# Attention ahead of two feed-forward stages: the weighted sums of half a sequence begin eight steps behind its first scores instead of nine

## The chip, the cores and the metric

The kernel runs on one core of a Trainium2 chip. The metric is the device time of one execution in microseconds (us); lower is better. Before the change the median of three runs is 1412.94 us (1412.52 to 1413.05).

## What is computed

Two batches of 768 tokens with 8 heads of 64 go through attention with a causal window of 128 keys and 4 sink keys, then through a dense feed-forward stage (512 to 2048 to 512), then through a mixture of eight experts (512 to 1024 to 512 each) whose weights come from a softmax that is balanced in eight rounds. Cut to what matters:

```python
scores = scale * np.matmul(q, k.transpose(0, 1, 3, 2))
scores = np.where(is_sink | in_window, scores, -1e9)
a = np.exp(scores - scores.max(-1)); a = a / (a.sum(-1) + 1e-9)
x = np.matmul(a, v)                      # attention, then to (1536, 512)
h = x @ w_in
x = (h * sigmoid(h)) @ w_out             # dense stage
P = balanced softmax of x @ w_gate       # eight rounds
out = sum over e of P[:, e] * (relu(x @ w1[e]) @ w2[e])
```

Only the attention and its passage into the dense stage are touched by the change; they fill about the first 160 us of the span.

## The kernel before

**Units, halves, steps.** Attention works on 8 units (a batch and a pair of heads) of 6 query tiles of 128 rows, so on 48 tiles in all (`NS`). Three consecutive tiles are a half, w = 0 to 15; a half is half of a unit's sequence, and even halves (g = 0) have three groups of keys, odd ones (g = 1) four. The loop at L325 in `banded` runs over steps s. Each step records, for several tiles at different stages, the instructions that all engines then run in the order recorded; no scheduler reorders them, and an engine that waits holds up everything recorded behind the wait on that engine.

**What a step records.** For tile s the scores of both heads on PE (`scores`, L236) and, on DVE, mask and row maximum (L240, two instructions and their read-outs). For tile s-1 the exponentials on ACT (L248). Then the weighted sums of an older half (`weighted`), one of its three parts per step. For tile s-2 the normalisation (`normalise`: L253 and L255 on DVE, L257 on POOL). For tile s-4 the transposes of the probabilities on PE (`turn`, L270). Where s is a multiple of 3, one more set of transposes for the sink keys of half s/3-2 (`turn_sinks`, L280). What PE wrote is then split in a high part (`highs`, ACT, L308) in the same step and a low part (`lows`, DVE, L313) in the next step; from step 48 on both come in the same step. The tiles are `tp` to `pt` for the probabilities, `ts` to `ss` for the sinks, `pv` to `xH` and `xL` for the result.

**The weighted sums.** Part 0 of half w opens an accumulation bank with the sinks' product (L292, which reads the whole of `ss`, high and low) and goes on with 6 matmuls (even halves) or 12 (odd halves) of 128x256; parts 1 and 2 have 6 each, and part 2 closes with the second sinks' product (L302). Each group of three matmuls (L111, L112, L113) is high by high, high by low, low by high. They read the values `vz`, which POOL splits four times per unit (`values`, L222 and L224), the first unit's at steps 4 to 7. Before the change part p of half w stands in step 3w+9+p.

**Beside it.** Steps 0 to 7 also record four idle transposes that keep PE at work (`warm_up`, L96). The generator `timeline` (L990) adds the preparation of the dense stage's weights: eight half chunks, each decoded over seven steps from step 7+5i on (`decode`, DVE L540, L541, L543; ACT L535, L545, L554; POOL L536, L547, L548, L555), and, around step 48, chunks of the second weight matrix. From step 48 on it also records blocks of the dense stage (`first`, tiles `pa`, twelve matmuls of 128x512, then L636 on ACT, L637 and L640 on DVE): blocks 0 to 3 of the first 512 tokens at steps 48 to 51, and blocks 0 to 2 of the second 512 tokens later. The latter read `xH` and `xL` of half 14, so they stand behind its part 2. With each block the planner's tasks go one stage on, and these put the decoding of the second matrix's chunks on DVE's queue between the blocks' own instructions.

```python
if s >= 9:
    late += weighted((s - 9) // 3, ii)
```

Of the kernel before, what the change touches and what calls it, by code (L numbers as in the profile page):

```python
# [26 lines left out]
def attn_ffn_moe_kernel(ctx, tc, q, k, v, n_sink, window, w_in, w_out, w_gate, w1, w2, out):  # L27
# [3 lines left out]
    NT = S // 128  # L31
# [19 lines left out]
    NU = len(units)  # L51
# [42 lines left out]
    def warm_up(ps, n):  # L94
        for _ in range(n):
            nc.tensor.transpose(ps[:, 0:128], ident, ident)  # L96
# [13 lines left out]
    def three(ps, sH, sL, mH, mL, first, last, **kw):  # L110
        nc.tensor.matmul(ps, sH, mH, start=first, stop=False, **kw)  # L111
        nc.tensor.matmul(ps, sH, mL, start=False, stop=False, **kw)  # L112
        nc.tensor.matmul(ps, sL, mH, start=False, stop=last, **kw)  # L113
# [35 lines left out]
    def banded(sp, experts):  # L149
# [36 lines left out]
        def masks():  # L186
            nc.vector.tensor_scalar(kp[:, prev], it[:, prev], wd, None, ALU.is_lt)
            nc.vector.tensor_scalar(mk[:, 1, own], kp[:, own], -1.0, -NEG, ALU.add, ALU.mult)
            nc.vector.tensor_tensor(mk[:, 1, prev], kp[:, prev], snk, ALU.max)
            yield  # L190
            nc.vector.tensor_scalar(mk[:, 1, prev], mk[:, 1, prev], -1.0, -NEG, ALU.add, ALU.mult)
            yield
            nc.vector.tensor_copy(kp[:, 128 : 128 + SK], snk[:, 0:SK])
            nc.vector.tensor_scalar(mk[:, 2], kp, -1.0, -NEG, ALU.add, ALU.mult)
# [32 lines left out]
        def scores(s):  # L227

            u, i = divmod(s, NT)
            res = []  # L230
            ps = [sp.bank(f"sc{s}_{h}", "sc")[:, :KW] for h in range(2)]
            qs = slice(128 * i, 128 * i + 128)
            ks = slice(160 * max(i - 1, 0), 160 * max(i - 1, 0) + KW)
            for h in range(2):
                d = slice(64 * h, 64 * h + 64)
                nc.tensor.matmul(ps[h], rq[u % 2][d, qs], rk[u % 2][d, ks], start=True, stop=True)  # L236
            for h in range(2):
                ng = ngs[(2 * s + h + 4) % 6]
                nm = sp.small.tile([128, 1], F32, name=f"nm{s}_{h}", tag="nm")
                nc.vector.tensor_tensor_reduce(ng, ps[h], mk[:, min(i, 2)], -SCALE, 3.0e38, ALU.add, ALU.min, nm)  # L240
                res.append((ng, nm))
            logits[s] = res

        def exponentials(s):
            pr = prs[s % 7]
            sm = sp.small.tile([128, 2], F32, name=f"sm{s}", tag="sm")
            for h, (ng, nm) in enumerate(logits.pop(s)):
                nc.scalar.activation(pr[:, :, h], ng, AF.Exp, bias=nm, scale=-1.0, accum_out=sm[:, h : h + 1])  # L248
            probs[s] = (pr, sm)

        def normalise(s):
            pr, sm = probs[s]
            nc.vector.tensor_scalar(sm, sm, 1.0e-9, None, ALU.add)  # L253
            yield
            nc.vector.reciprocal(sm, sm)  # L255
            for h in range(2):
                nc.gpsimd.tensor_scalar(pr[:, :, h], pr[:, :, h], sm[:, h : h + 1], 1.0, ALU.mult, ALU.mult)  # L257
# [26 lines left out]
        def weighted(w, part):  # L284

            u, g = divmod(w, 2)
            b, hp = units[u]
            pH, pL = pt[g]
            ms = [[[0], [1], [2]], [[0, 1], [2], [3]]][g][part]
            if part == 0:  # L290
                pos[w] = sp.bank(f"pv{w}", "pv")[:, :384]
                nc.tensor.matmul(pos[w], vs[0][:, u], sinks[w], start=True, stop=False)  # L292
            po = pos[w]
            for m in ms:
                j, t0 = prods[g][m]
                for h in range(2):
                    vH, vL = (x[:, j, 64 * h : 64 * h + 128] for x in vz[u % 2])
                    mH, mL = (x[:, h, 2 * m : 2 * m + 2].rearrange("p a b -> p (a b)") for x in (pH, pL))
                    three(po[:, 128 * t0 : 128 * t0 + 256], vH, vL, mH, mL, False, False, skip_group_check=True)
            if part < 2:  # L300
                return []
            nc.tensor.matmul(po, vs[1][:, u], sinks.pop(w), start=False, stop=True)  # L302
            c = slice(b * S + 384 * g, b * S + 384 * g + 384)
            return [(xH[hp][:, c], xL[hp][:, c], pos.pop(w))]
# [16 lines left out]
        NS = NT * NU  # L321
        late = []
        vals = iter(())
        setup = masks()
        for s in range(NS + 9):  # L325
            w, ii = divmod(s, 3)
            parts, late = late, []
            if s < NS:
                scores(s)
            if s < 8:  # L330
                warm_up(sp.bank("wt", "tr"), 4)
            next(setup, None)
            next(setup, None)
            if 0 <= s - 1 < NS:
                exponentials(s - 1)
            if s >= 9:
                late += weighted((s - 9) // 3, ii)
            nrm = normalise(s - 2) if 0 <= s - 2 < NS else iter(())
            next(nrm, None)
            lows(parts)  # L340
            next(nrm, None)
            if 0 <= s - 4 < NS:
                late += turn(s - 4)
            if ii == 0 and 0 <= w - 2 < 2 * NU:
                late += turn_sinks(w - 2)
            highs(late)
            if s >= NS:
                lows(late)
                late = []
            if s in (3, 4):  # L350
                c = slice(4 * s - 12, 4 * s - 8)
                nc.scalar.copy(vs[0][:, c], vsr[:, c])
                nc.gpsimd.tensor_tensor(vs[1][:, c], vsr[:, c], f32(vs[0][:, c]), ALU.subtract)
            if (s == 4 or s > 2 and s % 6 == 2) and s // 6 < NU:
                vals = values(s // 6)
            next(vals, None)
            if s % 6 == 0 and 0 < s and s // 6 + 1 < NU:
                load_unit(s // 6 + 1, "kq")
            if (s == 8 or s > 5 and s % 6 == 5) and s // 6 + 2 - (s == 8) < NU:
                load_unit(s // 6 + 2 - (s == 8), "v")  # L360
            next(experts)
# [609 lines left out]
    with tc.If(rvl != 0) as cmp:  # L971
        with tc.manual_schedule(), ExitStack() as st:
            sp = Space(st)
            ex = Experts(sp)
            ex.plan(True)

            halves = [words(sp.vsr, 512 * i, 512) for i in range(2)]
            tmp = [[words(sp.tm, 512 * i + 256 * c, 256) for c in range(2)] for i in range(2)]

            def load_half(i):  # L980
                c = 256 * (i // 2)
                nc.sync.dma_start(halves[i % 2].bitcast(I32).rearrange("p (k f) -> p k f", k=2), w_in.bitcast(I32)[:, c : c + 256].rearrange("(k p) f -> p k f", p=128)[:, 2 * (i % 2) : 2 * (i % 2) + 2])

            def decode_half(i):
                o = [words(t, 256 * (i % 2), 256, F32R) for t in ex.buffer("A", 0, i // 2)]
                yield from ex.decode(halves[i % 2], tmp[i % 2], o, True)
                if i + 2 < 8:
                    load_half(i + 2)

            def timeline():  # L990
                gens = {}
                for s in range(NT * NU + 9):
                    if s == 5:
                        load_half(0)
                        load_half(1)
                    for i in range(8):
                        at = s - 7 - 5 * i
                        if at == 0:
                            gens[i] = decode_half(i)
                        if at in (0, 1, 2, 3, 4, 5, 6):  # L1000
                            next(gens[i], None)
                    at = s - NT * NU
                    for a in (-6, -1, -1, 0):
                        if at == a:
                            ex.fetch()
                    if at == -3:
                        gens["Z"] = ex.prepare("Z", 0, 0)
                    if -3 <= at <= 1:
                        next(gens["Z"], None)
                    if at in (0, 1, 2, 3, 6, 7, 8):  # L1010
                        next(blocks)
                    yield

            blocks = ex.run(True)
            banded(sp, timeline())
            sp.cycle = ["sc"] * 3 + ["tr"] * 3
            for _ in blocks:
                pass
# [51 lines left out]
```

## Time and profile before

| what | value |
|---|---|
| median of the runs shown | 1412.94 us (1412.52 to 1413.05) |
| profiled execution: its own time | 1414.62 us |
| profiled execution: its span | 1412.8 us (1.8 us lie around it) |
| PE busy | 1399.0 us, 99% |
| DVE, ACT, POOL busy | 856.3, 537.0, 504.2 us (61, 38, 36%) |
| share of the chain of waits on PE | 96% |
| mean granted clock of PE | 0.996 |
| PE's waits over 0.5 us after the start | xL 2.2 us, once; vz L791 1.6 us, once; vz L790 1.0 us, twice |

How to read it: the span is that of the one execution that was profiled; the busy time of PE is modelled, because matmuls overlap, so a PE that looks busy may still be held up by short waits. In a timeline each line has the start, the length, the engine, the line of the kernel, what is written from what, how many instructions were merged, and in brackets how long the engine was idle before and what ended that. The distance from one PE line to the next is the time that its instructions really take up.

### The profile page before, as it was taken

The numbers are of one execution on the slowest core, as the hardware profiler recorded it, in microseconds if no ns is written. First come the engines' busy times: TensorE is split into PE (matmuls) and PEld (weight loads), VectorE is DVE, ScalarE is ACT, GpSimd is POOL, SyncE is SP. The second block draws the span as 40 slices with busy tenths as digits, with TensorE's granted clock in tenths as the row PEclk, the third lists the DMA queues.
The fourth block names the chain that finished last, engine by engine and source line by source line (L and its number), as shares of the span: only waits on it lengthen the run. The fifth ranks groups of instructions, "written<-read, shape, count | busy, mean of one in ns | idle before, by whom it ended". The sixth has DMA issues, their size and how long they took to land.

```text
span 1412.8 us, 18980 instructions
## 1 busy us (share of the span) xinstructions
PE 1399.0 (99%) x7065; PEld 1223.7 (87%) x7065; DVE 856.3 (61%) x1645; ACT 537.0 (38%) x1241; POOL 504.2 (36%) x657
## 2 busy tenths in 40 slices
PE   9999999999999999999999999999999999999998
PEld 6778788888878899989998998899899989989997
DVE  7989798786565756555455455545554554555454
ACT  6887333333345333333333333333333333332330
POOL 7887232232223233234333223432322343233230
PEclk9999999999999999999999999999999999999999
DMA  5341122211000100001000100100010011001002
GB/s 132 112 126 67 60 77 73 75 60 61 16 15 31 45 29 32 31 30 45 30 30 33 43 30 31 45 31 30 30 46 30 31 34 42 31 30 46 15 0 92
DMA packets 60293, 65.29 MB, mean 46 GB/s; under 512 B 10400, under 2 KB 47520, under 8 KB 60192
## 3 DMA queue, kind: packets, MB, share of 16 engines
q1 hardware_dynamic: 59904, 63.99, 14.0%
q8 instruction: 57, 0.93, 0.3%
q14 instruction: 44, 0.36, 0.1%
q10 hardware_dynamic: 288, 0.00, 0.0%
HBM read 60.84 MB, written 3.15 MB: 45 GB/s over the span
## 4 chain that ended last, share of the span: by engine, by line
PE 96%; DVE 1%; DMA 1%; POOL 1%; ACT 0%; SPq 0%; issue 0%; ACTq 0%; DVEq 0%
PE py L113 13%; PE py L112 12%; PE py L111 12%; PE pq L111 11%; PE pq L113 11%; PE pq L112 11%; PE pz L111 3%; PE pz L113 3%; PE pz L112 3%; PE pa L112 3%; PE pa L113 3%; PE pa L111 3%; PE sc L236 2%; PE tp L270 1%; PE pv L111 1%; PE pv L113 1%
## 5 line engine op out<-in xcount | busy, mean ns | idle before, releaser
L834 DVE SCALAR_TENSOR_TENSOR pr<-py,P,pr 128x512 f32<-128x512 f32 x224 | 168.1, 750 | 117.8 <-PE py L113 117.8
L113 PE MATMUL py<-pt,vz 128*128 128x512 f32 x576 | 226.2, 393 | 1.6 <-DVE vz L791 1.6
L111 PE MATMUL py<-pt,vz 128*128 128x512 f32 x576 | 225.2, 391 | 1.0 <-ACT vz L790 1.0
L112 PE MATMUL py<-pt,vz 128*128 128x512 f32 x576 | 225.5, 392 | 0.0
L787 DVE TENSOR_TENSOR mk<-pq,rqk 128x384 f32<-128x384 f32 x128 | 71.3, 557 | 214.4 <-PE pq L113 214.4
L571 POOL TENSOR_TENSOR pt<-ng,pt 128x256 fp32r<-128x256 f32 (+1 forms) x66 | 66.3, 1009 | 210.9 <-ACT pt L570 210.9
L571 POOL TENSOR_TENSOR pt<-rqk,pt 128x512 fp32r<-128x512 f32 (+1 forms) x50 | 55.0, 1101 | 225.6 <-ACT pt L570 225.5
L113 PEld LDWEIGHTS py<-pt,vz 128*128 128x128 f32 x576 | 108.3, 188 | 25.5 <-DVE vz L791 2.7
L111 PEld LDWEIGHTS py<-pt,vz 128*128 128x128 f32 x576 | 108.3, 188 | 21.9 <-ACT vz L790 1.6
L112 PEld LDWEIGHTS py<-pt,vz 128*128 128x128 f32 x576 | 108.2, 188 | 19.9
L794 ACT COPY rqk<-pq 128x384 f32<-128x384 f32 x64 | 30.7, 480 | 216.2 <-PE pq L113 216.2
L790 ACT ACTIVATE vz<-mk 128x384 fp32r<-128x384 f32 x128 | 66.9, 522 | 80.5 <-DVE mk L787 80.5
L791 DVE SCALAR_TENSOR_TENSOR vz<-mk,vz 128x384 fp32r<-128x384 f32 x128 | 72.0, 562 | 6.0 <-ACT vz L790 6.0
L112 PE MATMUL py<-pt,ss 128*128 128x512 f32 x192 | 74.9, 390 | 0.0
L111 PE MATMUL py<-pt,ss 128*128 128x512 f32 x192 | 74.6, 389 | 0.0
L636 ACT ACTIVATE mk<-pa 128x512 f32<-128x512 f32 x48 | 28.7, 598 | 101.3 <-PE pa L113 63.5
L834 DVE SCALAR_TENSOR_TENSOR tm<-py,P,tm 128x512 f32<-128x512 f32 x56 | 42.0, 751 | 32.6 <-PE py L113 32.6
L637 DVE TENSOR_TENSOR mk<-mk,pa 128x512 f32<-128x512 f32 x48 | 33.0, 687 | 43.0 <-ACT mk L636 42.9
L112 PE MATMUL pa<-xL,wa 128*128 128x512 f32 x144 | 56.7, 393 | 2.2 <-DVE xL L313 2.2
L257 POOL TENSOR_SCALAR pr<-pr,sm 128x288 f32<-128x288 f32 x96 | 51.9, 557 | 16.0 <-DVE sm L255 6.0
L570 ACT CAST pt<-ng 128x256 fp32r<-128x256 f32 (+1 forms) x66 | 33.5, 509 | 63.2 <-POOL ng L585 24.9
L111 PE MATMUL pa<-xH,wa 128*128 128x512 f32 x144 | 57.0, 396 | 0.0
(428 smaller groups left out, 3807.6 us busy)
## 6 DMA issues: line engine op xcount, KB each, us to landing
rqk<-in_moe_w_dram SPq DMA_DIRECT2D x32, 512.0 KB, 3.3
rv<-in_moe_w_dram SPq DMA_DIRECT2D x16, 512.0 KB, 3.4
ng<-in_moe_w_dram SPq DMA_DIRECT2D x16, 512.0 KB, 3.2
rqk<-in_moe_w_out_dram SPq DMA_DIRECT2D x8, 512.0 KB, 3.2
rv<-in_v_dram SPq DMA_DIRECT2D x8, 384.0 KB, 3.7
rqk<-in_moe_w_in_dram SPq DMA_DIRECT2D x6, 512.0 KB, 3.8
rqk<-in_k_dram SPq DMA_DIRECT2D x7, 384.0 KB, 5.1
rqk<-in_q_dram SPq DMA_DIRECT2D x7, 384.0 KB, 5.4
```

The source lines that it names most:

```text
L111: nc.tensor.matmul(ps, sH, mH, start=first, stop=False, **kw)
L112: nc.tensor.matmul(ps, sH, mL, start=False, stop=False, **kw)
L113: nc.tensor.matmul(ps, sL, mH, start=False, stop=last, **kw)
L257: nc.gpsimd.tensor_scalar(pr[:, :, h], pr[:, :, h], sm[:, h : h + 1], 1.0, ALU.mult, ALU.mult)
L570: nc.scalar.copy(o[0], src)
L571: nc.gpsimd.tensor_tensor(o[1], src, f32(o[0]), ALU.subtract)
L637: nc.vector.tensor_tensor(sg, sg, ps, ALU.mult)
L787: add = lambda o, x, y: nc.vector.tensor_tensor(o, x, y, ALU.add)
L790: nc.scalar.activation(oH, src, AF.Relu)
L791: nc.vector.scalar_tensor_tensor(oL, src, 0.0, f32(oH), ALU.max, ALU.subtract)
L794: nc.scalar.copy(self.p1, ps)
L834: nc.vector.scalar_tensor_tensor(o, ps, self.P[:, tt, e : e + 1], o, ALU.mult, ALU.add)
```

## The change

The loop over steps ends at step 55 instead of 56. Part p of half w moves from step 3w+9+p to step 3w+8+p. In `timeline` the three blocks of the second 512 tokens move from the 6th, 7th and 8th step after step 48 to the 5th, 6th and 7th.

```diff
-        for s in range(NS + 9):
+        for s in range(NS + 8):
...
-            if s >= 9:
-                late += weighted((s - 9) // 3, ii)
+            if s >= 8:
+                late += weighted(*divmod(s - 8, 3))
...
-                for s in range(NT * NU + 9):
+                for s in range(NT * NU + 8):
...
-                    if at in (0, 1, 2, 3, 6, 7, 8):
+                    if at in (0, 1, 2, 3, 5, 6, 7):
                         next(blocks)
```

No instruction is added or removed on any engine; SP's queue of transfers stands in the same order. PE and, with the results, ACT and DVE get another order. Three places on PE (names: `sc8_0` are the scores of tile 8 for head 0, `tp4` the transposes of tile 4, `pv0` the sums of half 0, `ss` the sinks; the number at the end is a buffer's).

Steps 8 and 9, where the sums begin, before:

```order
L236 MATMUL sc8_0_422<-rqk1_73 128x288
L236 MATMUL sc8_1_423<-rqk1_73 128x288
L270 MATMUL tp4_438<-ident_84,pr_155 128x128 x4
L236 MATMUL sc9_0_446<-rqk1_73 128x288
L236 MATMUL sc9_1_447<-rqk1_73 128x288
L292 MATMUL pv0_457<-ss_162,vs_159 128x384
L111 MATMUL pv0_457<-pt0_160,vz0_156 128x256
L112 MATMUL pv0_457<-pt0_160,vz0_156 128x256
L113 MATMUL pv0_457<-pt0_160,vz0_156 128x256
```

and now (the three matmuls per head stand twice, for two heads; the first head's are shown):

```order
L236 MATMUL sc8_0_422<-rqk1_73 128x288
L236 MATMUL sc8_1_423<-rqk1_73 128x288
L292 MATMUL pv0_433<-ss_162,vs_159 128x384
L111 MATMUL pv0_433<-pt0_160,vz0_156 128x256
L112 MATMUL pv0_433<-pt0_160,vz0_156 128x256
L113 MATMUL pv0_433<-pt0_160,vz0_156 128x256
...
L270 MATMUL tp4_446<-ident_84,pr_155 128x128 x4
L236 MATMUL sc9_0_454<-rqk1_73 128x288
L236 MATMUL sc9_1_455<-rqk1_73 128x288
```

The first part of half 0 has moved ahead of the transposes of tile 4 and the scores of tile 9.

The end of half 0 and the start of half 1, as it recurs for each half, before:

```order
L302 MATMUL pv0_457<-ss_162,vs_159 128x384
L270 MATMUL tp7_537<-ident_84,pr_155 128x128 x4
L236 MATMUL sc12_0_548<-rqk0_72 128x288
L236 MATMUL sc12_1_549<-rqk0_72 128x288
L292 MATMUL pv1_559<-ss_162,vs_159 128x384
```

and now:

```order
L302 MATMUL pv0_433<-ss_162,vs_159 128x384
L270 MATMUL tp6_514<-ident_84,pr_155 128x128 x2
L236 MATMUL sc11_0_522<-rqk1_73 128x288
L236 MATMUL sc11_1_523<-rqk1_73 128x288
L292 MATMUL pv1_533<-ss_162,vs_159 128x384
```

The sinks' product of half 1 stands behind the scores of tile 11 instead of those of tile 12, while the sinks it reads are still made by DVE between its work on tiles 10 and 11.

Around block 2 of the dense stage (`pa0_0_2`), before:

```order
L270 MATMUL tp46_1943<-ident_84,pr_155 128x128 x4
L111 MATMUL pa0_0_2_1952<-xH0_64,wa_149 128x512
...
L113 MATMUL pa0_0_2_1952<-xH3_67,wa_149 128x512
L292 MATMUL pv14_1975<-ss_162,vs_159 128x384
...
L270 MATMUL tp47_1983<-ident_84,pr_155 128x128 x4
```

and now:

```order
L292 MATMUL pv14_1945<-ss_162,vs_159 128x384
...
L270 MATMUL tp46_1953<-ident_84,pr_155 128x128 x4
L111 MATMUL pa0_0_2_1960<-xH0_64,wa_149 128x512
...
L113 MATMUL pa0_0_2_1960<-xH3_67,wa_149 128x512
```

Part 0 of half 14 has moved ahead of block 2. On DVE the order from this block's L637 to the low part of half 14's result (`xL_71`) and on is the same as before.

## Rows read from the trace of the kernel before

**Rows 1.** The page, part 1: busy us, share of the span, instructions.

```profile
PE 1399.0 (99%) x7065; PEld 1223.7 (87%) x7065; DVE 856.3 (61%) x1645; ACT 537.0 (38%) x1241; POOL 504.2 (36%) x657
```

**Rows 2.** Timeline of PE, steps 8 and 9: start us, length us, instruction, idle before.

```profile
23.52 0.76 PE L236 MATMUL sc<-rqk 64*128 64x288 f32 x4
...
26.05 0.44 PE L292 MATMUL pv<-ss,vs 128*128 128x384 f32 x1
...
27.36 0.39 PE L113 MATMUL pv<-pt,vz 128*128 128x256 f32 x1 [0.29 <-POOL vz L224]
27.59 0.66 PE L270 MATMUL tp<-ident,pr 128*128 128x128 f32 x4
```

**Rows 3.** Timeline of POOL, the split of the first unit's values, second head.

```profile
24.81 0.53 POOL L222 TENSOR_SCALAR vz<-rv 128x384 fp32r<-128x384 f32 x1
...
26.28 1.03 POOL L224 TENSOR_TENSOR vz<-rv,vz 128x384 fp32r<-128x384 f32 x1
```

**Rows 4.** Timeline of PE, steps 10 to 12.

```profile
28.50 0.76 PE L236 MATMUL sc<-rqk 64*128 64x288 f32 x4
29.19 0.39 PE L111 MATMUL pv<-pt,vz 128*128 128x256 f32 x1
...
30.01 0.41 PE L270 MATMUL tp<-ident,pr 128*128 128x128 f32 x2
30.35 0.76 PE L236 MATMUL sc<-rqk 64*128 64x288 f32 x4
31.04 0.38 PE L111 MATMUL pv<-pt,vz 128*128 128x256 f32 x1
...
32.03 0.63 PE L270 MATMUL tp<-ident,pr 128*128 128x128 f32 x4
32.58 0.76 PE L236 MATMUL sc<-rqk 64*128 64x288 f32 x4
33.27 0.44 PE L292 MATMUL pv<-ss,vs 128*128 128x384 f32 x1
```

**Rows 5.** Timeline of DVE, step 10: scores to sinks of half 1.

```profile
29.29 0.46 DVE L240 CUSTOM_DVE_ANT_0 ng<-sc,mk 128x288 f32<-128x288 f32 x1 [0.50 <-PE sc L236]
...
30.05 0.17 DVE L253 TENSOR_SCALAR sm<-sm 128x2 f32<-128x2 f32 x1
...
30.84 0.55 DVE L313 TENSOR_TENSOR ss<-ts,ss 64x384 fp32r<-64x384 f32 x1
```

**Rows 6.** Timelines of PE, POOL and DVE, steps 40 and 41: half 11.

```profile
103.16 0.76 PE L236 MATMUL sc<-rqk 64*128 64x288 f32 x4
...
102.89 1.00 POOL L224 TENSOR_TENSOR vz<-rv,vz 128x384 fp32r<-128x384 f32 x1
...
103.21 0.71 DVE L253 TENSOR_SCALAR sm<-sm 128x2 f32<-128x2 f32 x1
...
104.54 0.55 DVE L313 TENSOR_TENSOR ss<-ts,ss 64x384 fp32r<-64x384 f32 x1
```

**Rows 7.** Timeline of PE, scores of step 42.

```profile
105.40 1.26 PE L236 MATMUL sc<-rqk 64*128 64x288 f32 x4
```

**Rows 8.** Timeline of PE: behind block 2, and the first block of the second tokens.

```profile
133.32 0.33 PE L292 MATMUL pv<-ss,vs 128*128 128x384 f32 x1
...
134.21 0.65 PE L270 MATMUL tp<-ident,pr 128*128 128x128 f32 x4
...
145.66 0.50 PE L112 MATMUL pa<-xL,wa 128*128 128x512 f32 x1 [2.20 <-DVE xL L313]
```

**Rows 9.** Timeline of DVE: block 2's L637, and half 14's low part.

```profile
134.15 0.69 DVE L637 TENSOR_TENSOR mk<-mk,pa 128x512 f32<-128x512 f32 x1 [0.92 <-ACT mk L636]
...
145.06 0.55 DVE L313 TENSOR_TENSOR xL<-pv,xH 128x384 fp32r<-128x384 f32 x1
```

**Rows 10.** Busy us by stretch: PE, PEld, DVE, ACT, POOL, granted clock, DMA share, GB/s.

```profile
146.50:150.00 3.50, 3.50 (x13) 2.92 (x12) 2.88 (x4) 2.18 (x4) 2.33 (x2) 0.51 0.00 0
```

## Prediction

> **What bounds the kernel now.** I first read the table of engines on the page: PE is busy for 1399.0 us, 99% of the span [rows 1], and every other engine far less. The change removes no instruction, so it can win only what PE idles, and it loses whatever new idle time it makes. Then I read PE's timeline over the attention, to see where PE waits and for whom. Three places matter. At the start of the sums, in step 9, the sixth matmul of half 0 waits for POOL's last split of the values: it starts at 27.36, right behind the split's end at 26.28 + 1.03 = 27.31 [rows 2, 3]. In between, PE runs one instruction behind the other; the time of a piece is the distance between starts: scores 0.69, part 1 of a half 0.82, two transposes 0.34, part 2 of a half 0.99, four transposes 0.55 [rows 4]. Last, behind the mixed blocks, PE stands still for 2.20 us until DVE delivers half 14's low part [rows 8], and right after that the granted clock is 0.51 for 3.50 us [rows 10], which is the lower of its levels, 1.2 GHz. DVE's timeline tells why DVE is late there: it had waited 0.92 us before block 2's L637 at 134.15, worked from then on without a gap, and came to `xL` at 145.06 [rows 9]. So that stall's end is set by DVE's queue, counted from block 2.
>
> **The change part by part.**
>
> *The start of the sums: 1.24 us lost.* Part 0 of half 0 now stands in step 8, behind scores that start at 23.52 [rows 2]. It can begin at 23.52 + 0.69 = 24.21. Its second head needs the high values, ready at 24.81 + 0.53 = 25.34, and the last matmul needs the low values, ready at 27.31 [rows 3]. POOL's queue up to there holds only work on tiles whose scores came earlier, so it doesn't move. PE therefore ends part 0 at 27.59, as before. But before, the transposes of tile 4 and the scores of tile 9 were done by then, and now they come after: 0.55 + 0.69 = 1.24 us. Nothing hides this, as PE runs on without a gap afterwards. DVE gets tile 9's scores later too, and uses the time on nothing that PE waits for.
>
> *The start of each later half: 2.2 us lost (0.8 to 3.7).* L292 of half w reads `ss`, which DVE finishes behind the scores of tile 3w+7. For half 1 these scores start at 28.50, and `ss` is done at 30.84 + 0.55 = 31.39 [rows 4, 5]. Before, L292 came at 33.27 [rows 4], 1.88 us later. Now it stands behind the scores of tile 11, started at 30.35, and part 2 (0.99) has taken the place of part 1 (0.82) before it: 30.35 + 0.69 + 0.17 = 31.21, which is 0.18 us too early. The same reckoning over halves 1 to 13, each on its own rows, gives 4.15 us in all. Half 1 is the first of them, half 11 the worst: 103.16 + 0.86 = 104.02 against 104.54 + 0.55 = 105.09, 1.07 us short [rows 6]. Where DVE isn't behind, the odd halves are short by 0.18 as half 1 is and the even ones by nothing, so seven odd halves make 1.26 us. The rest is DVE being behind on decoding, and a wait on PE gives DVE time to catch up. Also, where DVE was behind, PE had paid already at the next scores, 1.26 - 0.76 = 0.50 us at step 42 [rows 7], and needn't pay twice. Bounds: 1.26 - 0.50 = 0.76 and 4.15 - 0.50 = 3.65. I take the middle, 2.2, because part of the lag goes. Behind the waiting L292 stand the matmuls of part 0, the transposes and the next scores, so DVE and ACT wait for it too.
>
> *Why DVE's pace is uncertain.* The small L253 ahead of `ss` took 0.17 us in step 10 and 0.71 in step 40 [rows 5, 6]; in the latter, POOL's L224 ran from 102.89 to 103.89 and L253 ended at 103.92 [rows 6]. The Trainium skill, page "SBUF — State Buffer", section "Who interferes with whom", says that the vector engine in a two-port mode and GpSimd exclude each other for a whole instruction, whoever is first. The trace agrees with it in that pair.
>
> *The tail: 0.89 us lost.* Part 0 of half 14 has moved ahead of block 2: from 133.32 to 134.21, 0.89 us [rows 8]. Block 2 ends that much later, and DVE's queue from block 2's L637 to `xL` stands in the same order, 145.06 + 0.55 - 134.15 = 11.46 us of work without a gap [rows 9]. The 0.92 us that DVE waited there grows, and `xL` comes 0.89 later. PE has less to do before it, so its stall grows from 2.20 to about 3.1 us. What PE does after the stall is the same as before. The step that falls away had no time of its own: its part of the sums is only run elsewhere.
>
> *The clock: 0.85 us lost (0 to 1.7).* The stall of 2.20 us was followed by 3.50 us at 0.51, which costs 0.49 x 3.50 = 1.7 us [rows 10]. The tail's stall should be followed by the same, so that costs nothing new; its bounds are 1.7 us either way, should it fall while PE stands or last twice as long. The new stall in step 8 is about 2.1 us in two pieces, the longer from about 25.6 to 27.36. It is a bit shorter than the row's and broken by two matmuls, so I take half of 1.7.
>
> *At nothing:* the three blocks of the second tokens, which keep their place behind half 14 and beside half 15; the earlier results `xH` and `xL`, which nobody waits for before step 48; transfers, in the same order. If DVE had been the bound in the attention, the earlier `xL` would shift its load too, but over three steps DVE does the same work.
>
> *Sum.* 1.24 + 2.2 + 0.89 + 0.85 = 5.2 us. The profiled execution took 1414.62 us (span 1412.8), 1.7 above the median of 1412.94. So it would be 1419.8 profiled, and 1412.94 + 5.2 = 1418.1 as a median, 0.37% slower. From about 160 us on PE works without slack, so nothing later takes it back.
>
> **The rivals.** (A) *The waits are absorbed.* DVE catches up after the first stall, L292 costs only the lower bound of 0.76, and the clock doesn't fall in step 8: 1.24 + 0.76 + 0.89 = 2.9 us; should the tail's fall in clock then cost 1 us less, 1414.8. For it: every wait of PE hands DVE time. Against it: DVE's path from scores to `ss` is latency, 31.39 - 28.50 = 2.89 us [rows 4, 5], which no slack shortens.
>
> (B) *Faster.* PE's rows look dense because the model stretches matmuls, and the steps are in truth paced by the other engines, each running ahead of PE by a step. Then a step less is a step's time less: 30.35 to 32.58, 2.2 us [rows 4], and half 14's low part comes before PE asks for it, which saves 2.20 and the 1.7 of the clock: 1412.94 - 6.1 = 1406.8. It decides at DVE: had DVE no gap before block 2's L637, its queue would be the pace, and `xL` would come earlier with the earlier step. The row shows a gap of 0.92 [rows 9], which speaks against it.
>
> (C) *Collisions on every half.* If PE's new rhythm puts L253 behind POOL each time, each of 13 halves pays 0.71 - 0.17 = 0.54 [rows 5, 6], 7.0 us more: 1425.1. The rule of the skill named above would make it so where POOL's instruction is always first. For it is that POOL and DVE then run in lockstep with PE; against it, that in step 10 POOL didn't hold L253 up.
>
> That the change doesn't do what it says is excluded: the order on PE shows the moved parts.
>
> **How the numbers follow.** Forecast 0.66, A 0.22, B 0.08, C 0.04. A measurement of this kernel can tell about 0.2% from no change, 2.8 us, so faster is below 1410.1 and slower above 1415.8. Forecast and C lie above, A on the whole within, B below: faster 0.08, same 0.22, slower 0.70. The forecast's own range goes from its lower bounds, 1.24 + 0.76 + 0.89 = 2.9, less 1.7 for the tail's clock, 1414.1, to its upper ones, 1.24 + 3.65 + 0.89 + 1.7 = 7.5 and 1.7 more for a longer fall in the tail, 1422.1. That takes in A, and leaves out B and C.
>
> **What would show it.** Right: L113 of half 0 waiting for `vz` L224 by about 1.7 us and ending at about 27.6; L292 waiting for `ss` at odd halves; the wait for `xL` with block 2's L637 behind an idle DVE. Wrong: no wait at L292, scores of step 42 starting at 105.40 or before [rows 7], or a stall for `xL` under 2.2 us.

## The result, and the profile after

The changed kernel takes 1420.96 us, the median of five runs (1419.93 to 1422.22). Beside it the kernel before took 1413.05 us (1412.52 to 1414.32). The ratio is 1.0055, with a 95% interval of 1.0044 to 1.0066: 0.55% slower, 7.9 us. The forecast of 1418.1 us had the sign, and its range of 1414.1 to 1422.1 holds the time; the cost was 7.9 us where 5.2 were worked out. The profiled execution took 1421.31 us, its span 1419.4.

The page of the changed kernel, the busy table and the first line of the chain of waits:

```profile
PE 1398.2 (99%) x7065; PEld 1223.0 (86%) x7065; DVE 858.1 (60%) x1645; ACT 536.5 (38%) x1241; POOL 503.9 (35%) x657
...
PE 94%; DVE 3%; DMA 1%; ACT 1%; issue 0%; SPq 0%; POOL 0%; ACTq 0%; DVEq 0%
```

The busy times are those of [rows 1]. On the chain of waits PE has lost 2 points of its 96%, and DVE stands there now with 3%. The list of PE's waits says for what (total us, times, longest us):

```profile
PE pv L292 <- DVE ss L313: 6.0, 10, 1.2
PE pa L112 <- DVE xL L313: 2.3, 1, 2.3
PE py L113 <- DVE vz L791: 1.6, 1, 1.6
...
PE pv L113 <- POOL vz L224: 1.4, 1, 1.4
...
PE pv L111 <- POOL vz L222: 0.4, 1, 0.4
```

The first line is new: L292 never waited over 0.5 us before. The wait for `xL` and the one for `vz` L791 were there before; the waits for L224 and L222 are those of step 8. The timeline of PE shows where they lie, here steps 8 to 11, and L292 of two later halves:

```profile
23.54 0.76 PE L236 MATMUL sc<-rqk 64*128 64x288 f32 x4
24.23 0.44 PE L292 MATMUL pv<-ss,vs 128*128 128x384 f32 x1
...
25.41 0.39 PE L111 MATMUL pv<-pt,vz 128*128 128x256 f32 x1 [0.40 <-POOL vz L222]
...
27.35 0.40 PE L113 MATMUL pv<-pt,vz 128*128 128x256 f32 x1 [1.44 <-POOL vz L224]
...
32.07 0.76 PE L236 MATMUL sc<-rqk 64*128 64x288 f32 x4
...
35.18 0.44 PE L292 MATMUL pv<-ss,vs 128*128 128x384 f32 x1 [0.36 <-DVE ss L313]
...
50.59 0.45 PE L292 MATMUL pv<-ss,vs 128*128 128x384 f32 x1 [0.97 <-DVE ss L313]
...
111.46 0.44 PE L292 MATMUL pv<-ss,vs 128*128 128x384 f32 x1 [1.16 <-DVE ss L313]
```

Three things differ from [rows 2] and [rows 4]. The last matmul of part 0 of half 0 still starts at 27.35, but PE stood before it for 1.44 us and 0.40 us. The scores of step 10 start at 32.07 instead of 28.50. And L292 waits for `ss` at its half: 0.36 us at half 1, 0.97 at half 3, 1.16 at half 11.

The first window below gives a part of why step 10 is so late: by its granted clock, PE ran at 0.52, the lower of its levels, 1.2 GHz, right after the stall in step 8. The second window is the one behind the stall in the tail, and answers to [rows 10]. Columns as in [rows 10].

```profile
27.50:31.00 3.50, 3.50 (x14) 2.41 (x15) 1.09 (x6) 1.64 (x5) 1.78 (x4) 0.52 0.40 112
153.50:157.50 4.00, 3.66 (x12) 3.20 (x13) 2.05 (x4) 2.25 (x4) 1.19 (x1) 0.57 0.00 0
```

The tail, DVE's timeline, then PE's stall, which answer to [rows 9] and [rows 8]:

```profile
142.34 0.69 DVE L637 TENSOR_TENSOR mk<-mk,pa 128x512 f32<-128x512 f32 x1 [1.28 <-ACT mk L636]
...
153.24 0.55 DVE L313 TENSOR_TENSOR xL<-pv,xH 128x384 fp32r<-128x384 f32 x1
```

```profile
153.84 0.77 PE L112 MATMUL pa<-xL,wa 128*128 128x512 f32 x1 [2.26 <-DVE xL L313]
```

Block 2's L637 is 8.19 us later than before and `xL` 8.18: DVE's queue between the two is the same length, as forecast. So all of the loss has been made by then. Where it was made can be counted on the starts of PE's scores:

- up to step 10: 32.07 - 28.50 = 3.57 us. Of this, 0.82 is part 1 of half 0, which now lies ahead of that point and is no loss. 2.75 us are.
- from step 10 to step 47: the scores there start at 125.11 instead of 117.94, 7.17 later. 0.99 is part 2 of half 12, moved ahead likewise. So 6.18 - 2.75 = 3.43 us were lost at halves 1 to 12.
- half 13: its L292 waits 0.97 us at 126.83, and some 0.1 more goes in starting again.
- block 2: 0.89, by the move alone.

The sum is 2.75 + 3.43 + 1.07 + 0.89 = 8.1 us, and the first matmul of the dense stage's second product starts 8.12 us later, at 165.76 instead of 157.64.

### The profile page after: what moved, and what is told of

It reads as the page before. It is cut to its first block, busy times and chain, and to the rows that moved or that the text cites. A ratio compares the mean times of both kernels' runs of the same rounds, so it can differ in the third digit from the quotient of the medians.

```text
span 1419.4 us, 18979 instructions
## 1 busy us (share of the span) xinstructions
PE 1398.2 (99%) x7065; PEld 1223.0 (86%) x7065; DVE 858.1 (60%) x1645; ACT 536.5 (38%) x1241; POOL 503.9 (35%) x657
## 3 DMA queue, kind: packets, MB, share of 16 engines
HBM read 60.84 MB, written 3.15 MB: 45 GB/s over the span
## 4 chain that ended last, share of the span: by engine, by line
PE 94%; DVE 3%; DMA 1%; ACT 1%; issue 0%; SPq 0%; POOL 0%; ACTq 0%; DVEq 0%
PE py L113 12%; PE py L112 12%; PE py L111 12%; PE pq L111 11%; PE pq L113 11%; PE pq L112 11%; PE pz L112 3%; PE pz L111 3%; PE pz L113 3%; PE pa L112 3%; PE pa L113 3%; PE pa L111 3%; PE sc L236 1%; PE tp L270 1%; PE pv L111 1%; PE pv L113 1%
## 5 line engine op out<-in xcount | busy, mean ns | idle before, releaser
L791 DVE SCALAR_TENSOR_TENSOR vz<-mk,vz 128x384 fp32r<-128x384 f32 x128 | 71.9, 562 | 6.0 <-ACT vz L790 6.0
L637 DVE TENSOR_TENSOR mk<-mk,pa 128x512 f32<-128x512 f32 x48 | 33.0, 687 | 43.5 <-ACT mk L636 43.5
```

The costliest lines, as they stand in the source:

```text
L637: nc.vector.tensor_tensor(sg, sg, ps, ALU.mult)
L791: nc.vector.scalar_tensor_tensor(oL, src, 0.0, f32(oH), ALU.max, ALU.subtract)
```

## The experiments

The theory was the prediction's: the start of the sums, the wait at L292, the tail and the clock add up. The rivals were that DVE is simply overloaded, so that an earlier step changes nothing in its pace; that the waits at L292 come from the shifted rhythm that the first stall made; and that the clock, not the waits, carries most of it. What DVE does in sum while PE waits speaks against an overload. The group of L240 (the first work on each tile's scores) shows the time that DVE stood idle until PE delivered scores, before and after (busy us, mean ns | idle us):

```profile
L240 DVE CUSTOM_DVE_ANT_0 ng<-sc,mk 128x288 f32<-128x288 f32 x75 | 31.0, 450 | 7.9 <-PE sc L236 7.7
```

```profile
L240 DVE CUSTOM_DVE_ANT_0 ng<-sc,mk 128x288 f32<-128x288 f32 x78 | 32.3, 451 | 13.3 <-PE sc L236 13.2
```

7.9 us before and 13.3 after (28 to 125 us): in sum DVE has become idler, and PE waits for it nevertheless. (At single halves DVE was late all the same; the part on the prediction shows one.) So what counts is how long `ss` comes behind a half's last scores, and "sinks first" shortens that. Each kernel was timed 5 to 12 times, beside the kernel before on the same chip.

**Half 0 late.** The three parts of half 0 stay in steps 9 to 11; all others are eight behind.

```diff
-            if s >= 8:
-                late += weighted(*divmod(s - 8, 3))
+            for p in ([s - 9] if 9 <= s < 12 else []) + ([s - 8] if s >= 11 else []):
+                late += weighted(*divmod(p, 3))
```

> The changed kernel, but half 0 keeps its old place (parts at steps 9, 10, 11); all later halves stay one step earlier. Theory (three separate losses: the start of the sums 1.24 us of order and 1.5 us of clock, the waits of L292 about 4.4 us, the tail 0.9 us): the wait for the values in step 8 and the fall of the clock behind it go, so 2.7 us less than the changed kernel's 1421.0, 1418.2, some 5.2 us above the kernel before; L292's waits in the later halves stay near 6 us in sum. Rival (DVE is the pace, and the start only shifts where the delay shows): the time stays at 1421 within 0.7 us, with longer waits at L292 of half 1 and 2.

Measured: 1418.1 us (1416.83 to 1420.37) against 1414.32 for the kernel before, which the next three are set against as well; ratio to before 1.0036 (1.0023 to 1.0049). Its two waits in the attention:

```profile
PE pv L292 <- DVE ss L313: 5.7, 9, 1.2
...
PE pv L113 <- POOL vz L224: 0.3, 1, 0.3
```

The stall in step 8 is gone, and with it some 2.9 us against the changed kernel. L292 waits nearly as much as before the edit, 5.7 us instead of 6.0: these waits are not a consequence of the first stall.

**Sinks first.** DVE makes the low part of `ss` ahead of that of the other tiles of its step, and ACT the high part last, as it did.

```diff
-            if ii == 0 and 0 <= w - 2 < 2 * NU:
-                late += turn_sinks(w - 2)
-            highs(late)
+            sk = turn_sinks(w - 2) if ii == 0 and 0 <= w - 2 < 2 * NU else []
+            highs(late + sk)
+            late = sk + late if s < NS else late + sk
```

> The changed kernel, but before step 48 DVE makes the low part of the sinks ahead of that of the probabilities; no other engine's order moves. Theory (L292 is held by DVE's latency from the scores to the sinks): the sinks are done about 0.65 us sooner, ten waits of 6.0 us in sum shrink to under 1.5 us, and the time falls by about 4 us to 1417. Rival (DVE is simply loaded to its limit by the moved results, so the wait moves to the scores' banks or the probabilities): waits of L292 go but as much appears at L236 or L111, and the time stays within 1 us of 1421.

Measured: 1415.87 us (1412.82 to 1418.53), ratio 1.0013 (1.0004 to 1.0023). The waits, then DVE's work for half 1 in step 11:

```profile
PE pv L292 <- DVE ss L313: 0.6, 1, 0.6
```

```profile
35.73 0.55 DVE L313 TENSOR_TENSOR ss<-ts,ss 64x384 fp32r<-64x384 f32 x1
36.31 0.69 DVE L313 TENSOR_TENSOR pt<-tp,pt 128x512 fp32r<-128x512 f32 x1
```

`ss` now precedes `pt`, and every wait at L292 of halves 1 to 14 is gone; the 0.6 us left are half 15's, in the tail. DVE does the same work in another order, so the place of `ss` in its queue decided: from the start of a half's last scores to the end of `ss` it is now 2.3 to 2.8 us, against 2.9 to 3.9 in the changed kernel (halves 1 to 13). The edit does more than put `ss` ahead by one instruction: the rhythm moved too, and L253 at halves 3, 11 and 13 took 0.30, 0.24 and 0.16 us instead of 0.96, 0.71 and 0.95. The median falls by 5.1 us (5.9 by the two ratios). What should remain is the 2.75 us of the start and the 0.89 of the tail, less 1.97 for waits at scores that the kernel before had (last but one experiment): 1.7 us, and 1415.87 - 1414.32 = 1.6 are measured. That they agree so well is in part luck, as the median lies in a gap between two groups of runs.

The single runs fall in two groups: six from 1412.8 to 1414.8 us, six from 1417.0 to 1418.5. The mean granted clock divides them: 0.997 or 0.998 in the lower six, 0.994 to 0.996 in the upper. The profile is of one at the top, and its clock was low for longer than the changed kernel's:

```profile
28.00:32.00 4.00, 4.00 (x16) 2.91 (x17) 1.51 (x8) 1.63 (x5) 1.68 (x4) 0.50 0.38 105
32.00:36.00 4.00, 4.00 (x22) 2.71 (x20) 1.88 (x10) 2.24 (x7) 2.22 (x3) 0.68 0.01 2
```

**Keep the clock.** The changed kernel with twelve more idle transposes in step 8, which PE runs in the time in which it would wait for the values.

```diff
-            if s < 8:
-                warm_up(sp.bank("wt", "tr"), 4)
+            if s < 9:
+                warm_up(sp.bank("wt", "tr"), 4 if s < 8 else 12)
```

> The changed kernel with 12 idle transposes more in step 8, between the scores and the sums, which fill about 1.5 us of the 2.1 us that PE would stand still. Theory (the stall in step 8 also cost the clock): the granted clock stays 1.00 behind 27.6 us, the end of part 0 of half 0 stays at 27.6, and the time falls by 1.5 us to 1419.5. Rival (the clock falls but PE is not what paces there, so it costs nothing): the clock stays up and the time stays within 0.5 us of 1421.

Measured: 1420.88 us (1420.5 to 1421.7), ratio 1.0053 (1.004 to 1.0066): nothing gained on the changed kernel's 1420.96. Yet the clock stayed up:

```profile
27.50:31.00 3.50, 2.99 (x21) 2.48 (x22) 1.39 (x6) 1.66 (x5) 2.36 (x5) 1.00 0.42 123
```

The timeline of PE tells where the gain went. The first line here is step 8, the others step 10, half 1, and step 47:

```profile
24.22 0.76 PE L236 MATMUL sc<-rqk 64*128 64x288 f32 x4
...
31.23 0.76 PE L236 MATMUL sc<-rqk 64*128 64x288 f32 x4
...
34.88 0.44 PE L292 MATMUL pv<-ss,vs 128*128 128x384 f32 x1 [0.89 <-DVE ss L313]
...
125.34 0.76 PE L236 MATMUL sc<-rqk 64*128 64x288 f32 x4
```

and this is DVE's L253 ahead of half 1's `ss`:

```profile
32.77 0.88 DVE L253 TENSOR_SCALAR sm<-sm 128x2 f32<-128x2 f32 x1
```

This execution lies 24.22 - 23.54 = 0.68 us behind the changed kernel's at step 8 already. At step 10 it is ahead by 0.84 + 0.68 = 1.52 us, and at step 47 by 0.68 - 0.23 = 0.45. Most of what the clock gave at the start, the waits at L292 took: half 1 waits 0.89 us instead of 0.36, and the sum over the waits is 7.2 us instead of 6.0. The 1.2 us more stand at halves 1, 9 and 10, and in each L253 took longer than in the changed kernel: 0.88, 0.51 and 0.64 us against 0.34, 0.17 and 0.29. At half 1 it ends at 33.65, when POOL's L224 has just ended, at 33.62. So the gain was lost to other meetings of DVE and POOL in the moved rhythm. One profiled execution shows this; that it must go so isn't shown, though the five runs agree that nothing was gained.

**Sinks first in the kernel before.** The same edit as in "sinks first", on the kernel before.

> The kernel before, with the same swap on DVE as in e2_sinks_first. Control: with L292 nine steps behind, the sinks were early by 0.4 to 2.75 us already, so theory and rival both say no change: 1413.0 within 0.7 us. If it gains over 1.5 us, the swap helps for another reason than L292's wait, and e2 can't be read as that.

Measured: 1413.23 us (1411.3 to 1414.89), ratio 0.9996 (0.9988 to 1.0005). No change, so the gain of 5.1 us above is the removal of waits that the earlier step made, and not a general merit of the order.

**Tail alone.** Parts 0 to 41 stay nine steps behind, those from half 14 on are eight behind.

```diff
-            if s >= 8:
-                late += weighted(*divmod(s - 8, 3))
+            for p in ([s - 9] if 9 <= s < 51 else []) + ([s - 8] if s >= 50 else []):
+                late += weighted(*divmod(p, 3))
```

> The kernel before, with only the end of the change: the sums of halves 14 and 15 (from part 0 of half 14 on) one step earlier, and one step less; halves 0 to 13 stay nine behind. Theory (block 2 of the dense stage comes later by the moved part, and DVE's queue behind it sets when half 14's low part is ready): block 2 ends 0.9 us later, low part of half 14 about 0.9 us later, PE's idle before it (L292 of half 15 included) 2.2 + 0.9 = 3.1 us, the time 0.9 us above the kernel before. Rival (a step less at the end is a gain, and the tail of the changed kernel is late only because all before it is late): stall under 2.2 us, the time 0.5 to 2 us below the kernel before.

Measured: 1413.77 us (1412.19 to 1416.69) against 1413.52, ratio 1.0001 (0.9992 to 1.001): the time can't tell 0.9 us from nothing. The trace can. Its attention lies 0.50 us ahead of the profiled kernel before (step 47 at 117.44), and then, on DVE:

```profile
134.53 0.69 DVE L637 TENSOR_TENSOR mk<-mk,pa 128x512 f32<-128x512 f32 x1 [1.76 <-ACT mk L636]
...
145.43 0.55 DVE L313 TENSOR_TENSOR xL<-pv,xH 128x384 fp32r<-128x384 f32 x1
```

With the 0.50 added, L637 is 0.88 and `xL` 0.87 later than in [rows 9], with DVE idle for 1.76 instead of 0.92 us before L637. PE stands for 0.58 us at half 15's L292 and for 2.28 at `xL`, 2.86 together.

**Half 0 late and sinks first together.** Both edits above, on the changed kernel.

> The changed kernel with both repairs: half 0 at its old place, and the low part of the sinks first on DVE. Theory: the start and the waits of L292 are gone, only the tail's 0.9 us is left, and PE needn't wait at the scores' banks where the kernel before did (about 1 to 2 us): within 1.5 us of the kernel before, 1413. Rival (DVE's load is the limit, wherever the wait shows): 2 us or more above the kernel before, with waits at other lines between 30 and 125 us.

Measured: 1413.33 us (1410.49 to 1415.35) against 1413.52, ratio 0.9998 (0.9989 to 1.0007). With the start and L292 mended, the shorter lag costs nothing; the waits left in the attention are those of the tail (0.58 and 2.27 us).

**Block 3 late.** The kernel before, with the last block of the first tokens moved into the tail: it stands where PE stalls for `xL`.

```diff
-                    if at in (0, 1, 2, 3, 6, 7, 8):
+                    if at in (0, 1, 2, 5, 6, 7, 8):
                         next(blocks)
```

> The kernel before, with block 3 of the dense stage recorded two steps later, behind the step in which half 14's result is split; so the low part stands on DVE ahead of the decoding that block 3 sets going. Theory (DVE's queue behind block 2 sets the stall): the 2.2 us stall of PE before the block of the second tokens is gone, with it the fall of the clock behind it (1.7 us), and the time falls by about 3.9 us to 1409. Rival (PE runs out of work between blocks 2 and 3, or later blocks wait for the second matrix's chunks, decoded later): a stall of about 2 us at L292 or at pz, and no change.

Measured: 1410.51 us (1409.11 to 1412.35), ratio 0.9975 (0.9965 to 0.9984), 3.0 us faster than before. The windows of the tail, of the kernel before and of this one:

```profile
138.00:146.00 8.00, 5.80 (x38) 5.00 (x37) 7.37 (x13) 1.59 (x3) 0.00 (x0) 1.00 0.00 0
146.00:154.00 8.00, 8.00 (x35) 6.79 (x34) 5.78 (x7) 4.05 (x8) 3.86 (x3) 0.79 0.35 101
```

```profile
138.00:146.00 8.00, 8.00 (x45) 6.96 (x44) 7.34 (x14) 1.10 (x2) 0.00 (x0) 1.00 0.00 0
146.00:154.00 8.00, 8.00 (x39) 6.56 (x39) 6.21 (x7) 3.80 (x8) 3.15 (x3) 1.00 0.38 116
```

PE is busy throughout, and its clock stays at 1.00. Less is gained than the 3.9 us expected, which count a fall of the clock behind the stall in every run of the kernel before; at one mean granted clock the gain is nearer the stall's 2.2 us (0.999: 1409.11 us against 1411.3 to 1411.7). On DVE the distance from block 2's L637 to `xL` has shrunk to 5.05 us, from 10.91 in [rows 9]: the planner's tasks that came along with block 3 now stand behind `xL`.

```profile
134.39 0.69 DVE L637 TENSOR_TENSOR mk<-mk,pa 128x512 f32<-128x512 f32 x1 [0.94 <-ACT mk L636]
...
139.44 0.56 DVE L313 TENSOR_TENSOR xL<-pv,xH 128x384 fp32r<-128x384 f32 x1
```

**All three.** Half 0 late, sinks first, and, in the tail of the changed kernel, block 3 a step later, at the fourth step after step 48 instead of the third:

```diff
-                    if at in (0, 1, 2, 3, 5, 6, 7):
+                    if at in (0, 1, 2, 4, 5, 6, 7):
                         next(blocks)
```

> The changed kernel with both repairs of e6 and block 3 recorded behind the split of half 14's result as in e7. Theory: the stall at the end goes too, so it is 3 to 4 us faster than e6 and beats the kernel before, 1409 to 1410; against e7 it has a step less and no more to gain from it, so they are within 1 us. Rival (the shorter lag is worth a step's time once its waits are gone): 2 us or more faster than e7.

Measured: 1408.04 us (1407.58 to 1410.16), ratio 0.9961 (0.9947 to 0.9974). This is below both kernels, 5.5 us below the kernel before, and 2.5 below "block 3 late", to which it adds the shorter lag. What the lag gives stands in the starts of PE's scores. Steps 42 and 43 in the kernel before, where DVE was behind with reading the scores' banks ([rows 7] has the first line's 105.40):

```profile
109.20 0.76 PE L236 MATMUL sc<-rqk 64*128 64x288 f32 x4
```

and in this kernel:

```profile
105.74 0.76 PE L236 MATMUL sc<-rqk 64*128 64x288 f32 x4
...
108.14 0.76 PE L236 MATMUL sc<-rqk 64*128 64x288 f32 x4
```

Step 42 takes 2.40 us instead of 3.80. Steps 21 and 36 have gone from 3.15 and 4.20 to 2.41 and 2.40 as well. Part of these differences is work that changed its step (a step of this kind took 2.58 or 3.30 us before where it didn't stall); the rest is 0.57 + 0.90 + 0.50 = 1.97 us of stalls that the kernel before paid at these scores. The list of PE's waits has little left at L292, 0.47 us at half 13, where L253 takes 1.05 us, and 0.60 at half 15:

```profile
PE pv L292 <- DVE ss L313: 1.1, 2, 0.6
```

So about 1 us is left to the lag, not 2.5. Runs at one mean granted clock say the same: at 0.999 they take 1408.03 and 1408.04 us here and 1409.11 in "block 3 late", at 0.998 1409.35 and 1410.16 against 1410.1 to 1410.65. The rest of the 2.5 us lies in how often the clock fell in the few runs of each, so the rival's gain of 2 us or more isn't shown.

**Sinks first, clock kept.** To find what divides the runs of "sinks first" in two groups, the idle transposes of "keep the clock" were added to it.

> The changed kernel with the low part of the sinks first (as e2) and the 12 idle transposes in step 8 (as e3). In e3 the clock stayed up and nothing was gained; in e2 the twelve runs fell in two groups, seven of 1412.8 to 1414.8 us at a mean clock of 0.997 or 0.998 and five of 1417.0 to 1418.5 at 0.994 to 0.996. Theory (a lost clock costs nothing while DVE paces the attention, and its full price once L292 no longer waits): no run above 1416, median 1414, a clock of 0.997 or more in every run. Rival (the two groups come from somewhere else, as the fall at the end): two groups again, at least one run in four above 1416.5.

Measured: 1414.26 us (1412.13 to 1417.07) against 1414.07, ratio 1.0004 (0.9995 to 1.0013). Two of twelve runs lie above 1416 us where six did without the transposes, so neither the theory (none) nor the rival (at least one in four) was met. (The expectation counts seven and five runs in the two groups of "sinks first"; they are six and six.) That part of the upper group was the clock in step 8 is suggested, and with twelve runs each not shown. The profiled run took 1417.07 us and kept its clock at the start (1.00 from 27.5 to 31 us). It lost it behind the tail's stall, in the window below, and again behind the one at `vz` L791, where it was 0.68 from 410 to 420 us.

```profile
140.00:150.00 10.00, 7.31 (x34) 6.21 (x35) 8.17 (x15) 3.00 (x6) 1.00 (x1) 0.86 0.00 0
```

So falls elsewhere put runs into the upper group too. Whether the clock at the start costs time in a kernel where L292 doesn't wait stays open, and so does what decides in which runs it falls.

## Why the prediction was right, and which term was too small

**The start of the sums, 1.24 us: right.** The last matmul of part 0 of half 0 starts at 27.35 after waits of 1.44 and 0.40 us, the forecast having been about 1.7 and an end at 27.6. Leaving half 0 in its place gave 2.9 us back, the order's 1.24 and the 1.5 of the clock.

**The clock, 0.85 (0 to 1.7): the fall came, at 1.5 us**, 2.75 less the 1.24. But it isn't a term that can be taken away by itself. Held up, it moved the total by 0.08 us, as L253 was then held up longer and L292 waited 1.2 us more. The prediction added the two terms as if neither moved the other.

**The start of each later half, 2.2 us (0.76 to 3.65): the mechanism right, the size wrong, and outside its bounds.** This is the step that failed. The idle times at L292 of halves 1 to 13 add up to 5.42 us in nine waits, 0.9 more goes in starting again after them, and 1.97 us of stalls at scores that the kernel before had are saved: 4.4 us, which is the 3.43 and 1.07 counted above within 0.2. The prediction's count over the rows of before gave 4.15 gross where 5.42 came (half 11 short by 1.07 there, 1.16 in the trace after). It put starting again at nothing, and the stalls saved at 0.50 where they were 1.97. It then took the middle, "because part of the lag goes", and a wait on PE lets DVE catch up. In sum DVE did become idler, but the lag did not go. The prediction says against rival A that the path to `ss` is latency which no slack shortens, and halved the term all the same.

What the 5.42 us are can be read from the rows of DVE after. From the start of a half's last scores to the end of `ss` it is 2.9 us where nothing delays DVE, and then the odd halves are 0.18 short, as the prediction has it: about 1.2 us. Some 1.5 us more come where DVE takes up these scores late, at halves 6, 8 and 11 (1.58, 1.10 and 1.23 us behind their start, 0.79 otherwise). There it was still decoding, so the rival of an overloaded DVE has a part in it. At half 6, PE's scores of step 25, then DVE, which starts on them without having been idle:

```profile
70.05 0.76 PE L236 MATMUL sc<-rqk 64*128 64x288 f32 x4
...
70.87 0.84 DVE L541 SCALAR_TENSOR_TENSOR tm<-vsr,tm 128x256 int32<-128x256 int32 x1
71.64 0.44 DVE L240 CUSTOM_DVE_ANT_0 ng<-sc,mk 128x288 f32<-128x288 f32 x1
```

The remaining 2.7 us are L253 taking longer than its 0.17 us. So all odd halves did not wait alike, as supposed, and two even ones waited too (0.81 us at half 6, 0.33 at half 8). The three worst are 3, 11 and 13, and in each the small L253 ahead of `ss` was held up by POOL. For half 3, POOL's and DVE's timelines in step 17:

```profile
48.34 1.00 POOL L224 TENSOR_TENSOR vz<-rv,vz 128x384 fp32r<-128x384 f32 x1
```

```profile
48.40 0.96 DVE L253 TENSOR_SCALAR sm<-sm 128x2 f32<-128x2 f32 x1
...
49.99 0.55 DVE L313 TENSOR_TENSOR ss<-ts,ss 64x384 fp32r<-64x384 f32 x1
```

L253 takes 0.96 us here, against 0.17 in [rows 5], and ends at 49.36 when L224 ends at 49.34. `ss` follows at 50.54, and L292 starts at 50.59. For half 13 it is 0.95 us behind an L224 of 1.00. The Trainium skill, page "SBUF — State Buffer", section "Who interferes with whom", states that of a vector instruction in a two-port mode and a GpSimd one the first to start holds the shared ports for its whole length, and the other is blocked. The trace agrees in these ends, within 0.02 us; in which mode L253 runs no row shows. So the mechanism of rival C is real, and sits in its full size in three halves, not in thirteen; a split of L224 in shorter pieces, which would show how much of the wait is its doing, wasn't tried.

**The tail, 0.89 us: right.** It is 0.88 in the experiment on the tail alone. The stall of PE, forecast at 3.1, is 2.26 us at `xL` and 0.58 at half 15's L292, 2.84 together; that the second part would stand at another instruction wasn't foreseen.

**The rivals.** A (absorbed, 1414.8) fell with the idle times at L292. B (faster, 1406.8) had the wrong cause: DVE's idle time before block 2's L637 grew from 0.92 to 1.28 us, as the prediction held against it, and `xL` did not come early. But a time near B's is reached, 1408.0, where the new waits are taken away one by one and block 3 is moved, which alone gives 3.0 us in the kernel before.

**The sum.** Worked out: 1.24 + 2.2 + 0.89 + 0.85 = 5.2. Found: 1.24 + 4.4 + 0.89 + 1.5 = 8.0, against 7.9 by the medians. That the time lies in the range is in part luck: without the 1.7 us that its upper end allows for a longer fall of the clock in the tail, which did not come, the end is 1412.94 + 7.5 = 1420.4, below the 1420.96. Profiled spans differ by less, 6.6 us, for a reason that has nothing to do with the change. Both kernels stall for 1.58 us at `vz` L791, about 250 us after the attention. Of the kernel before, PE's wait and the two windows at it:

```profile
413.07 0.80 PE L113 MATMUL py<-pt,vz 128*128 128x512 f32 x1 [1.58 <-DVE vz L791]
```

```profile
410.00:415.00 5.00, 2.67 (x7) 1.66 (x8) 3.88 (x7) 1.20 (x3) 2.14 (x2) 0.78 0.33 108
415.00:420.00 5.00, 5.00 (x25) 3.48 (x24) 0.00 (x0) 2.21 (x6) 1.47 (x2) 0.88 0.00 0
```

and of the changed kernel, where the same wait is at 421.17:

```profile
420.00:425.00 5.00, 3.83 (x20) 2.95 (x21) 1.99 (x3) 1.52 (x4) 2.00 (x3) 1.00 0.02 6
425.00:430.00 5.00, 5.00 (x29) 3.48 (x28) 0.00 (x0) 2.20 (x7) 3.35 (x5) 1.00 0.00 0
```

The granted clock fell to 0.78 and 0.88 in the one and stayed at 1.00 in the other: 0.22 x 5 + 0.12 x 5 = 1.7 us, which is the difference between 8.1 and 6.6 within 0.2. A median carries such falls as well. Of the 25 runs of the kernel before that were timed beside "block 3 late", the three at a mean granted clock of 0.999 took 1411.3 to 1411.7 us, the ten at 0.998 took 1412.6 to 1413.5, and the twelve at 0.995 to 0.997 took 1414.1 to 1416.0; so differences of 1 or 2 us between medians are read with that in mind.

## What to carry to other kernels

When a stage of a software pipeline is begun a step earlier, count for each of its inputs the time from its first cause to its last split against the step's length. A count of shortfalls from the rows shouldn't be discounted because the engine gets idle time elsewhere: here the shortfalls grew, from 4.15 to 5.42 us, as the engine was late at some halves and held up by another engine at others. If the count comes out short, look first at what stands ahead of the late input on its engine; putting the small input first cost nothing and took away nearly all of the waits. And terms added up from one trace aren't always gains that can be had one by one: a repair moves the rhythm, and with it which instructions meet (here the clock, held up, gained 1.5 us at the start and nothing in the end). Follow such a gain through the trace to the end.

## What the runs showed of the hardware

- A stall of 1.4 to 2.3 us is followed by a lower granted clock in some executions and not in others. Behind the same 1.58 us wait at `vz` L791 it fell in one profiled execution and not in the next. Behind the stall of 2.26 us at `xL` it fell in that of the changed kernel (0.57 from 153.5 to 157.5 us), and behind the same stall of 2.27 us it didn't in that of "half 0 late" (1.00 from 150.5 to 154.5).
- A fall of the clock to 0.52 for 3.5 us cost 1.5 us by step 10, yet the kernel that kept its clock there was no faster in the end (1420.96 and 1420.88 us). Within one kernel the mean granted clock goes with the time: in "sinks first" the six runs at 0.994 to 0.996 lie about 3 us above the six at 0.997 and 0.998.
- A DVE instruction on 128x2 elements, 0.17 us by itself, takes up to 0.96 us in the changed kernel, and 1.05 in "all three", where a POOL instruction of 1.00 us runs beside it, and ends within 0.03 us of that one's end.
